# Attention with expert layers on one core: V's high and low parts as one 128-column moving operand, summed by VectorE

## The chip, the cores and the metric

The kernel runs on one core of a Trainium2 chip. The metric is the device time of one execution in microseconds; a comparison takes the median of several runs. A profile is one execution taken by the hardware profiler. Its engines are TensorE (PE, with its weight loads as PEld), VectorE (DVE), ScalarE (ACT), GpSimd (POOL) and SyncE (SP), which here issues the DMAs.

## The reference

Attention over 4 batches of 8 heads, 576 positions and 64 values a head, with a position bias from a small network, and then a two-layer network on the result of all heads side by side (the expert layers).

```python
scores = scale * np.matmul(q, k.transpose(0, 1, 3, 2))
...
scores = scores + bias.transpose(2, 0, 1)[None, :, :, :]
scores = scores - np.max(scores, axis=-1, keepdims=True)
attn = np.exp(scores)
attn = attn / (np.sum(attn, axis=-1, keepdims=True) + 1e-09)
return np.matmul(attn, v).astype(np.float32)
...
h = np.maximum(x @ w_in, 0.0)
return (h * h @ w_out).astype(np.float32)
```

All inputs and the output are float32.

## The kernel before

**Tiling.** Two batches are worked on together (b = 0, 1), so p = 0, 1 is the pair of batches. The query rows of a pair are cut into five blocks c: c = 1 to 4 hold 128 rows of each batch, c = 0, the tail, the last 64 rows of both. A step is one (p, c, h): one head of one block. There are 80 steps, in the order of blocks in ORDER; the first two blocks, (0, 0) and (0, 3), work in float32 (f32c), the other eight in fp16. To keep the accuracy of float32 with fp16 matmuls, each operand is split into a high and a low part, and a product is the sum of three: high times high, high times low, low times high.

**A step of an fp16 block.** qk forms the scores of the head in the PSUM tile sc (L361 for the tail, L367 and L373 otherwise). softmax_a adds the bias and takes the row maximum on VectorE (L388, the score pass), and ScalarE takes the exponential (L394). softmax_b makes the fp16 parts a (high on ScalarE, low on POOL, L420 and L421), 1152 columns a batch: 576 high, 64 low of the last 64 keys and 512 low. A transposing DMA (L423) turns them into at, nine tiles of 128 keys a batch; the fifth holds high and low parts of the last 64 keys together. at and a have two buffers each.

**The product with V** (pv, L442 to L471) comes LAG = 3 steps later. V of a head is v_t, two planes: z = 0 high, z = 1 low, each with five tiles of 128 keys a batch and 64 columns. For each batch half there are 14 matmuls (L458), each with a weight load of its own: tiles 0 to 4 of at times high V and times low V, tiles 5 to 8 times high V. All go to the same 64 columns of the PSUM tile pv, which is one bank (ps_pv has one buffer) and is full after four heads. Then VectorE evacuates it (L470): it multiplies the four heads of each batch half by the reciprocal of the sums and writes x, the 512 columns of all heads. finish_x, at the end of a block, scales x, splits it into fp16 parts xh, and a transposing DMA makes xt.

**The expert layers** of a block are eight units. g1 (L512) is 24 matmuls with 256 columns (128 for the tail) into hp, followed by ScalarE, VectorE and POOL work (L518 to L522); g2 (L535) is 12 matmuls with 512 columns (6 for the tail) into o. They run inside the steps of later blocks, one unit a step, and after the last step for the rest. In the first half, the bias tables are made between them: hg (L282 on VectorE, some on ScalarE), its matmuls bp (L309) and their copies be.

**Order.** Each step calls qk, softmax_a, softmax_b, an expert unit and pv of an earlier head. A scheduler then orders each engine's instructions, and each engine takes its own in that order; the DMAs stand in one queue (SPq).

Of the kernel before, what the change touches and what calls it, by code (L numbers as in the profile page):

```python
# [49 lines left out]
def tile_attention_moe(  # L50
# [11 lines left out]
    nc = tc.nc  # L62
# [366 lines left out]
    def pv(p, c, h):  # L429
        at = st_.pop((p, c, h, "t"))  # L430
        f32 = (p, c) in f32c
        vt = v32[h].rearrange("p (j d) -> p j d", d=D) if f32 else v_t[p, h].rearrange("p z (j d) -> p z j d", d=D)
        if h % 4 == 0:
            pv_t[p, c] = ps_pv.tile([128, 512], F32, tag="pv", name="pv")
        po = pv_t[p, c]
        nb = 2 if c else 1
        for b in range(2):
            if c:
                o = ((h % 4) * 2 + b) * 64
                dst = po[:, o:o + 64]  # L440
            else:
                o = (h % 4) * 64  # L442
                dst = po[64 * b:64 * b + 64, o:o + 64]
            if f32:
# [9 lines left out]

            terms = [(blk, z, blk) for blk in range(5) for z in range(2)] + [(5 + blk, 0, blk) for blk in range(4)]
            for n, (ab, vz, blk) in enumerate(terms):
                lhsT = at[:, 9 * b + ab, :] if c else at[:, ab, 64 * b:64 * b + 64]
                nc.tensor.matmul(out=dst, lhsT=lhsT, rhs=vt[:, vz, 5 * b + blk, :], start=(n == 0), stop=(n == 13),  # L458
                                 tile_position=(0, 0 if c else 64 * b))
        if h % 4 == 3:  # L460
            h0 = h - 3
            if h0 == 0:
                x_t[p, c] = x_p.tile([128, 2, DM], F32, tag="x", name="x")
            x = x_t[p, c]
            su = sums[p, c]
            rd = sm2.tile([128, 4, 2], F32, tag="rd", name="rd")
            nc.scalar.activation(out=rd[:, :, 0:nb], in_=su[:, h0:h0 + 4, 0:nb], func=AF.Identity, bias=eps)
            nc.vector.reciprocal(out=rd[:, :, 0:nb], in_=rd[:, :, 0:nb])
            for b in range(nb):
                nc.vector.tensor_tensor(  # L470
                    out=x[:, b, h0 * 64:h0 * 64 + 256].rearrange("p (h d) -> p h d", d=D),  # L471
                    in0=pv_t[p, c].rearrange("p (h b d) -> p h b d", h=4, d=D)[:, :, b, :] if c
                    else pv_t[p, c][:, 0:256].rearrange("p (h d) -> p h d", d=D),
                    in1=rd[:, :, b:b + 1].to_broadcast([128, 4, D]), op=ALU.mult)
            pv_t.pop((p, c))

# [291 lines left out]
```

## Time and profile before

| what | value |
|---|---|
| runs shown | 692.01, 698.78 and 703.85 us, median 698.78 |
| the profiled execution | 692.05 us, of which span 690.3 |
| mean granted TensorE clock | 0.951 |
| PE busy | 626.1 us, 91% of the span |
| DVE busy | 415.6 us, 60% |
| ACT, POOL busy | 384.9 and 354.0 us, 56% and 51% |
| chain that ended last | PE 69%, DMA 12%, DVE 8%, issue 4% |

A busy share is over the whole span, and stages differ; the windows give it by stretch. A matmul's printed duration reaches to its modelled end and overlaps with the next, so what a run of matmuls costs is read from the starts. The chain of work is followed back from the last instruction, each step to what released it.

### The profile page before, as it was taken

How to read it: one execution, taken by the hardware profiler on the slowest of the kernel's cores; microseconds unless marked ns; L12 is line 12 of the kernel's file. 1: busy time of each engine (PE TensorE's matmuls, PEld its weight loads, DVE VectorE, ACT ScalarE, POOL GpSimd, SP SyncE). 2: the span in 40 equal slices, each digit the busy share in tenths (PEclk: the TensorE clock that was granted, in tenths of full speed). 3: DMA queues.
4: the chain of work that ended last, by engine and by line, in shares of the span. 5: the costliest groups of instructions: out<-in, count | busy, mean ns of one | idle time of the engine just before them, and what ended most of it. 6: DMA issues, size and time to landing. Idle time of an engine off the chain costs nothing.

```text
span 690.3 us, 15578 instructions
## 1 busy us (share of the span) xinstructions
PE 626.1 (91%) x6048; PEld 402.7 (58%) x6048; DVE 415.6 (60%) x830; ACT 384.9 (56%) x854; POOL 354.0 (51%) x369
## 2 busy tenths in 40 slices
PE   4087668899989999999999999999987999999997
PEld 1044335677555555666666676666664766676664
DVE  7458898998966694577657543436448446424120
ACT  6286666778866465765755633445575656431211
POOL 3416544587646445656865644445555664632221
PEclk9586787999999999999999999999998999999999
DMA  8868876576897677899998886459699779451000
GB/s 294 230 190 249 259 230 195 174 210 189 189 203 166 139 171 161 186 197 210 224 183 133 163 168 122 109 104 169 130 207 185 157 144 162 85 120 31 31 1 31
DMA packets 207721, 112.17 MB, mean 162 GB/s; under 512 B 168224, under 2 KB 184608, under 8 KB 207648
## 3 DMA queue, kind: packets, MB, share of 16 engines
q1 hardware_dynamic: 207648, 111.19, 69.9%
q8 instruction: 47, 0.77, 0.5%
q14 instruction: 26, 0.21, 0.1%
HBM read 55.44 MB, written 15.61 MB: 103 GB/s over the span
## 4 chain that ended last, share of the span: by engine, by line
PE 69%; DMA 12%; DVE 8%; issue 4%; ACT 3%; POOL 2%; SPq 0%; DVEq 0%; ACTq 0%; POOLq 0%
PE hp L512 23%; PE o L535 23%; PE pv L458 6%; DMA at<-a 6%; PE sc L373 5%; PE bp L309 3%; PE pv L451 3%; DMA stg<-kd 3%; DVE hg L282 2%; DMA xt<-xh 1%; PE tp L406 1%; PE sc L367 1%; PE sc L361 1%; DMA stg<-w_out 1%; DVE s L388 1%
## 5 line engine op out<-in xcount | busy, mean ns | idle before, releaser
L512 PE MATMUL hp<-xt,winH 128*128 128x256 f16 (+1 forms) x1280 | 195.8, 263 | 1.9 <-DMA xt<-xh 1.9
L535 PE MATMUL o<-woutH,g 128*128 128x512 f16 x576 | 186.2, 382 | 0.6 <-ACT o L542 0.6
L512 PE MATMUL hp<-xt,winL 128*128 128x256 f16 (+1 forms) x640 | 162.0, 262 | 0.0
L512 PEld LDWEIGHTS <-winH 128*128 128x128 f16 x1280 | 116.2, 98 | 36.5 <-issue 17.7
L535 PEld LDWEIGHTS <-g 128*128 128x128 f16 x864 | 83.5, 98 | 92.5 <-issue 8.9
L520 DVE TENSOR_TENSOR r<-hp,r 128x512 f32<-128x512 f32 (+1 forms) x80 | 50.7, 634 | 133.8 <-ACT r L518 133.8
L421 POOL TENSOR_TENSOR a<-s,a 128x1024 f16<-128x1024 f32 (+1 forms) x64 | 130.1, 2032 | 0.0
L522 POOL TENSOR_TENSOR g<-r,g 128x512 f16<-128x512 f32 (+1 forms) x80 | 86.4, 1080 | 80.6 <-DVE g L127 78.4
L388 DVE CUSTOM_DVE_ANT_0 s<-sc,bt 128x576 f32<-128x576 f32 x144 | 103.4, 751 | 38.7 <-PE sc L373 24.9
L394 ACT ACTIVATE s<-s,nm 128x576 f32<-128x576 f32 x144 | 111.4, 774 | 6.9
L535 PE MATMUL o<-woutL,g 128*128 128x512 f16 x288 | 110.0, 382 | 0.0
L392 ACT ACTIVATE nm<-mx,esc 128x1 f32<-128x1 f32 x144 | 41.1, 286 | 120.9 <-DVE mx L388 120.7
L420 POOL TENSOR_TENSOR a<-s,a 128x128 f16<-128x128 f32 (+1 forms) x64 | 28.3, 442 | 141.9 <-ACT a L123 130.6
L123 ACT ACTIVATE a<-s 128x1152 f16<-128x1152 f32 (+1 forms) x64 | 70.5, 1102 | 51.7 <-DMA at<-a 50.4
L518 ACT ACTIVATE r<-hp 128x512 f32<-128x512 f32 (+1 forms) x80 | 43.1, 538 | 60.1 <-PE hp L512 60.0
L458 PEld LDWEIGHTS <-at 128*128 128x128 f16 (+1 forms) x1792 | 60.6, 100 | 23.7 <-issue 8.2
L282 DVE TENSOR_SCALAR hg<-tab_t,nb 128x464 f32<-128x464 f32 (+17 forms) x102 | 62.4, 665 | 9.8 <-PE bp L309 9.6
L458 PE MATMUL pv<-v,at 128*128 128x64 f16 (+1 forms) x1792 | 64.4, 194 | 3.9 <-DMA at<-a 3.9
L512 PEld LDWEIGHTS <-winL 128*128 128x128 f16 x640 | 62.7, 98 | 6.4 <-issue 0.4
L309 PE MATMUL bp<-hg,w2s 128*32 128x288 f32 (+17 forms) x352 | 48.1, 547 | 9.1 <-ACT be L325 5.0
L373 PE MATMUL sc<-k,q 64*128 64x512 f16 x384 | 54.8, 391 | 0.0
L451 PEld LDWEIGHTS pv<-v,at 128*64 128x64 f32 (+3 forms) x320 | 36.1, 181 | 16.8 <-issue 10.7
(71 smaller groups left out, 674.4 us busy)
## 6 DMA issues: line engine op xcount, KB each, us to landing
bt<-biasd SPq DMA_DIRECT2D x64, 288.0 KB, 3.3
stg<-w_in SPq DMA_DIRECT2D x16, 512.0 KB, 4.3
stg<-w_out SPq DMA_DIRECT2D x16, 512.0 KB, 4.5
stg<-kd SPq DMA_DIRECT2D x16, 288.0 KB, 3.9
bt<-biasd SPq DMA_DIRECT2D x32, 144.0 KB, 3.4
qst<-qd SPq DMA_DIRECT2D x32, 128.0 KB, 3.3
out<-o SPq DMA_DIRECT2D x16, 256.0 KB, 2.4
v<-vd SPq DMA_DIRECT2D x8, 320.0 KB, 7.4
```

The source lines that it names most:

```text
L123: nc.scalar.activation(out=out, in_=in_, func=AF.Copy, scale=scale)
L282: nc.vector.tensor_scalar(ht, tab_t[:, 0:dlen(G)], scl[:, n:n + 1], nb1, op0=ALU.mult, op1=ALU.max)
L309: nc.tensor.matmul(out=bp[32 * t:32 * t + 32, 0:d1 - d0], lhsT=w2s, rhs=ts_[t][:, d0:d1], start=True, stop=True, tile_position=(0, 32 * t))
L373: nc.tensor.matmul(out=sc[:, 1024 * b:1024 * b + 512], lhsT=qt[r, qz, qs], rhs=kt[r, z, 64 * b:64 * b + 512], start=(n == 0), stop=(n == 2 ...
L388: nc.vector.tensor_tensor_reduce(s[:, 576 * b:576 * b + 576], sc[:, 960 * b:960 * b + 576], bt, inv, -3.0e38, ALU.add, ALU.max, mx[:, b:b ...
L394: nc.scalar.activation(out=sl, in_=sl, func=AF.Exp, bias=nm[:, b:b + 1], accum_out=su[:, h, b:b + 1])
L421: nc.gpsimd.tensor_tensor(av[:, :, 640:1152], ev[:, :, 0:512], av[:, :, 0:512], op=ALU.subtract)
L451: nc.tensor.matmul(out=dst, lhsT=lhsT, rhs=vt[r, 5 * b + blk, :], start=(blk == 0), stop=(blk == 4), tile_position=(0, 0 if c else 64 * b))
L458: nc.tensor.matmul(out=dst, lhsT=lhsT, rhs=vt[:, vz, 5 * b + blk, :], start=(n == 0), stop=(n == 13), tile_position=(0, 0 if c else 64 * b))
L512: nc.tensor.matmul(out=hp[:, f * T:f * T + T].rearrange("p (b t) -> p b t", b=nb), lhsT=wt[:, k, c0:c0 + 128], rhs=xt[:, 0:nb, z * 4 + k, ...
L522: nc.gpsimd.tensor_tensor(g[:, 1, 0:2 * T], r[:, 0:2 * T], g[:, 0, 0:2 * T], op=ALU.subtract)
L535: nc.tensor.matmul(out=blk["o"][b], lhsT=g[:, z, c0:c0 + 128], rhs=wt[:, 2 * u + f, :], start=(u == 0 and f == 0 and z == 0 and wt is wout ...
```

## The change

In the fp16 blocks, the high and the low part of a tile of V are one moving operand of 128 columns (two pieces of 64). Tiles 0 to 4 of at are each loaded once and multiplied with both; the result is two planes of 64 columns side by side. Tiles 5 to 8 go to the first plane as before. So a batch half has 9 matmuls in place of 14: 5 with 128 columns and 4 with 64. A head takes twice the room in the PSUM tile pv, whose bank is now full after two heads. After each second head, VectorE adds the two planes while it moves them to x (the new tensor_reduce, one for each batch half), and after four heads the multiplication by the reciprocal sums runs on x in place, from SBUF. The tile x is taken at the second head of a block in place of the fourth. The two float32 blocks work as before.

```diff
--- before.py
+++ after.py
@@ -430,17 +430,19 @@
         at = st_.pop((p, c, h, "t"))
         f32 = (p, c) in f32c
         vt = v32[h].rearrange("p (j d) -> p j d", d=D) if f32 else v_t[p, h].rearrange("p z (j d) -> p z j d", d=D)
-        if h % 4 == 0:
+
+        nh, w = (4, D) if f32 else (2, 2 * D)
+        if h % nh == 0:
             pv_t[p, c] = ps_pv.tile([128, 512], F32, tag="pv", name="pv")
         po = pv_t[p, c]
         nb = 2 if c else 1
         for b in range(2):
             if c:
-                o = ((h % 4) * 2 + b) * 64
-                dst = po[:, o:o + 64]
+                o = ((h % nh) * 2 + b) * w
+                dst = po[:, o:o + w]
             else:
-                o = (h % 4) * 64
-                dst = po[64 * b:64 * b + 64, o:o + 64]
+                o = (h % nh) * w
+                dst = po[64 * b:64 * b + 64, o:o + w]
             if f32:
                 for blk in range(5):
                     r = slice(0, 128 if blk < 4 else 64)
@@ -452,27 +454,42 @@
                                      tile_position=(0, 0 if c else 64 * b))
                 continue
 
-            terms = [(blk, z, blk) for blk in range(5) for z in range(2)] + [(5 + blk, 0, blk) for blk in range(4)]
-            for n, (ab, vz, blk) in enumerate(terms):
-                lhsT = at[:, 9 * b + ab, :] if c else at[:, ab, 64 * b:64 * b + 64]
-                nc.tensor.matmul(out=dst, lhsT=lhsT, rhs=vt[:, vz, 5 * b + blk, :], start=(n == 0), stop=(n == 13),
-                                 tile_position=(0, 0 if c else 64 * b))
+            for n in range(9):
+                lhsT = at[:, 9 * b + n, :] if c else at[:, n, 64 * b:64 * b + 64]
+                pos = (0, 0 if c else 64 * b)
+                if n < 5:
+                    nc.tensor.matmul(out=dst.rearrange("p (z d) -> p z d", z=2), lhsT=lhsT, rhs=vt[:, :, 5 * b + n, :],
+                                     start=(n == 0), stop=(n == 8), tile_position=pos)
+                else:
+                    nc.tensor.matmul(out=dst[:, 0:D], lhsT=lhsT, rhs=vt[:, 0, 5 * b + n - 5, :],
+                                     start=False, stop=(n == 8), tile_position=pos)
+        if h == (3 if f32 else 1):
+            x_t[p, c] = x_p.tile([128, 2, DM], F32, tag="x", name="x")
+        x = x_t[p, c] if (p, c) in x_t else None
+        if not f32 and h % 2 == 1:
+
+            for b in range(nb):
+                src = po.rearrange("p (h b z d) -> p h b d z", h=2, b=2, z=2)[:, :, b, :, :] if c else \
+                    po[:, 0:256].rearrange("p (h z d) -> p h d z", h=2, z=2)
+                nc.vector.tensor_reduce(x[:, b, (h - 1) * 64:(h + 1) * 64].rearrange("p (h d) -> p h d", d=D), src,
+                                        axis=AX.X, op=ALU.add)
+            pv_t.pop((p, c))
         if h % 4 == 3:
             h0 = h - 3
-            if h0 == 0:
-                x_t[p, c] = x_p.tile([128, 2, DM], F32, tag="x", name="x")
-            x = x_t[p, c]
             su = sums[p, c]
             rd = sm2.tile([128, 4, 2], F32, tag="rd", name="rd")
             nc.scalar.activation(out=rd[:, :, 0:nb], in_=su[:, h0:h0 + 4, 0:nb], func=AF.Identity, bias=eps)
             nc.vector.reciprocal(out=rd[:, :, 0:nb], in_=rd[:, :, 0:nb])
             for b in range(nb):
-                nc.vector.tensor_tensor(
-                    out=x[:, b, h0 * 64:h0 * 64 + 256].rearrange("p (h d) -> p h d", d=D),
-                    in0=pv_t[p, c].rearrange("p (h b d) -> p h b d", h=4, d=D)[:, :, b, :] if c
-                    else pv_t[p, c][:, 0:256].rearrange("p (h d) -> p h d", d=D),
-                    in1=rd[:, :, b:b + 1].to_broadcast([128, 4, D]), op=ALU.mult)
-            pv_t.pop((p, c))
+                xo = x[:, b, h0 * 64:h0 * 64 + 256].rearrange("p (h d) -> p h d", d=D)
+                if not f32:
+                    xi = xo
+                elif c:
+                    xi = po.rearrange("p (h b d) -> p h b d", h=4, d=D)[:, :, b, :]
+                else:
+                    xi = po[:, 0:256].rearrange("p (h d) -> p h d", d=D)
+                nc.vector.tensor_tensor(out=xo, in0=xi, in1=rd[:, :, b:b + 1].to_broadcast([128, 4, D]), op=ALU.mult)
+            pv_t.pop((p, c), None)
 
     moe = deque()
     blocks = {}
```


On TensorE the matmuls of a head stand as one run before and after, and from the fourth head of the second fp16 block on the runs follow each other almost as before: scores of a head, g1, g2, product with V of an earlier head. Only heads 6 and 7 of a block (in the last block heads 4 and 5) stand with at most scores between them. In the first fp16 block, (0, 2), expert units and bias matmuls are placed otherwise: between its heads 1 and 2 there now stand a score product, six matmuls of g2 and four of bp, where there were a score product, six of g2 and none.

VectorE, first place: around head 3 of the first fp16 block (L388 is the score pass on sc, hg the bias tables, r the first layer's result, x from pv the evacuation). Before:

```order
L282 TENSOR_SCALAR hg<-tab_t,nb_131 128x576 x3
L388 ISA s,mx<-sc,bt 128x576
L388 ISA mx 128x1
L388 ISA s,mx<-sc,bt 128x576
L388 ISA mx 128x1
L470 TENSOR_TENSOR x<-pv,rd 128x256
L520 TENSOR_TENSOR r<-hp,r 128x512
L470 TENSOR_TENSOR x<-pv,rd 128x256
L388 ISA s,mx<-sc,bt 128x576
L388 ISA mx 128x1
```

After, with the lines of the changed kernel (L474 is the new reduce, L491 the multiplication, L537 the former L520):

```order
L388 ISA s,mx<-sc,bt 128x576
L388 ISA mx 128x1
L282 TENSOR_SCALAR hg<-tab_t,nb_131 128x576 x3
L474 TENSOR_REDUCE x<-pv 128x128 x2
L537 TENSOR_TENSOR r<-hp,r 128x512
L491 TENSOR_TENSOR x<-x,rd 128x256 x2
L388 ISA s,mx<-sc,bt 128x576
L388 ISA mx 128x1
L388 ISA s,mx<-sc,bt 128x576
L388 ISA mx 128x1
```

The reduce stands behind the bias tables of 576 columns and ahead of r, and both multiplications stand ahead of the score passes, where they stood on both sides of r.

VectorE, second place: the end of the block (1, 1), while the scores of the tail block are at work (ax, cc and xh belong to finish_x). Before:

```order
L388 ISA s,mx<-sc,bt 128x576
L388 ISA mx 128x1
L470 TENSOR_TENSOR x<-pv,rd 128x256 x2
L487 TENSOR_REDUCE ax<-x 128x2
L489 TENSOR_SCALAR ax<-ax 128x1 x2
L490 RECIPROCAL cc<-ax 128x2
L495 TENSOR_SCALAR xh<-x,cc 128x512
L388 ISA s,mx<-sc,bt 128x576
L388 ISA mx 128x1
L496 SCALAR_TENSOR_TENSOR xh<-x,cc,xh 128x512
```

After:

```order
L388 ISA s,mx<-sc,bt 128x576
L388 ISA mx 128x1
L474 TENSOR_REDUCE x<-pv 128x128 x2
L491 TENSOR_TENSOR x<-x,rd 128x256 x2
L504 TENSOR_REDUCE ax<-x 128x2
L506 TENSOR_SCALAR ax<-ax 128x1 x2
L388 ISA s,mx<-sc,bt 128x576
L388 ISA mx 128x1
L507 RECIPROCAL cc<-ax 128x2
L512 TENSOR_SCALAR xh<-x,cc 128x512
L537 TENSOR_TENSOR r<-hp,r 128x512
```

The reduces were put in ahead of the multiplications, and the score pass that stood after xh now stands ahead of it.

## Rows read from the trace of the kernel before

**Rows 1.** windows by engine, columns named in the first line, 180 to 625 us
```profile
core 0: us, PE busy (x) PEld busy (x) DVE busy (x) ACT busy (x) POOL busy (x), PEclk, DMA share, GB/s
180.00:260.00 80.00, 76.32 (x783) 43.26 (x780) 60.60 (x110) 51.75 (x116) 40.48 (x37) 1.00 0.79 174
345.00:505.00 160.00, 160.00 (x1704) 107.13 (x1703) 79.30 (x171) 82.66 (x179) 84.64 (x87) 1.00 0.75 145
505.00:535.00 30.00, 24.16 (x332) 15.67 (x330) 21.34 (x45) 18.21 (x44) 16.58 (x15) 0.93 1.00 193
535.00:625.00 90.00, 90.00 (x960) 62.52 (x959) 41.44 (x94) 46.73 (x99) 45.70 (x38) 0.98 0.65 128
```

**Rows 2.** TensorE's timeline: start, duration, engine, line, operation; one step of the second half
```profile
491.05 0.98 PE L458 MATMUL pv<-v,at 128*128 128x64 f16 x28
491.86 0.33 PE L367 MATMUL sc<-kz,q 128*128 128x128 f16 x3
492.13 0.82 PE L373 MATMUL sc<-k,q 64*128 64x512 f16 x6
492.88 0.28 PE L512 MATMUL hp<-xt,winH 128*128 128x128 f16 x2
...
494.23 0.38 PE L535 MATMUL o<-woutH,g 128*128 128x512 f16 x1
...
496.82 0.57 PE L458 MATMUL pv<-v,at 128*128 128x64 f16 x14
```

**Rows 3.** the chain of work, piece by piece: start, duration, what; two heads in a row
```profile
607.67 1.63 PE pv L458 x56
```

**Rows 4.** TensorE's groups by form: busy us, mean ns of one, idle before
```profile
L458 PE MATMUL pv<-v,at 128*128 128x64 f16 x1568 | 56.6, 193 | 3.9 <-DMA at<-a 3.9
L458 PE MATMUL pv<-v,at 128*64 128x64 f16 x224 | 7.8, 198 | 0.0
```

**Rows 5.** TensorE's timeline, one head of the tail block
```profile
421.62 0.97 PE L458 MATMUL pv<-v,at 128*64 128x64 f16 x28
422.52 0.91 PE L361 MATMUL sc<-k,q 128*128 128x512 f16 x6
```

**Rows 6.** VectorE's groups by form, the evacuation and the reduces
```profile
L470 DVE TENSOR_TENSOR x<-pv,rd 128x256 f32<-128x256 f32 x36 | 13.8, 416 | 6.8 <-PE pv L458 6.7
L487 DVE TENSOR_REDUCE ax<-x 128x2 f32<-128x1024 f32 x8 | 9.7, 1216 | 0.2
L487 DVE TENSOR_REDUCE ax<-x 128x1 f32<-128x512 f32 x2 | 1.4, 686 | 0.1
```

**Rows 7.** VectorE's timeline at the end of a block
```profile
410.68 0.74 DVE L470 TENSOR_TENSOR x<-pv,rd 128x256 f32<-128x256 f32 x2
411.45 1.22 DVE L487 TENSOR_REDUCE ax<-x 128x2 f32<-128x1024 f32 x1
```

**Rows 8.** waits of the DMA queue: us in total, times, longest
```profile
SPq L423 <- PE pv L458: 68.4, 28, 4.9
```

**Rows 9.** the chain of work at the end of the first fp16 block
```profile
251.29 0.98 DVE xh L496
252.38 3.08 DVE hg L282 x3
255.46 3.13 DMA xt<-xh
...
259.99 3.25 DMA xt<-xh
...
263.29 2.79 PE hp L512 x24
```

**Rows 10.** the chain of work at a later block end
```profile
522.83 3.62 DMA xt<-xh
...
527.87 2.60 DVE xh L496
530.47 0.67 DVE s L388
...
532.36 1.40 PE sc L373 x6
```


## Prediction

> **What bounds the kernel now.** I read the windows first: per stretch of the span, how long each engine was busy. From 345 to 505 us and from 535 to 625 us TensorE is busy 100% of the time at full granted clock or nearly so, and VectorE 50% and 46% [rows 1]. These 250 us hold most of the products with V that the change rewrites. From 180 to 260 us (the first block in fp16, while bias tables are still made) VectorE is at 76% and TensorE leaves 3.7 us of 80 idle; from 505 to 535 us TensorE leaves 5.8 us of 30 idle and VectorE is at 71% [rows 1]. So what counts is TensorE's time per head, and VectorE's only in those two stretches.
>
> Next, TensorE's timeline of one step [rows 2]. The product with V of a head starts at 491.05 us, the scores of a later head at 491.86, 24 matmuls of the first expert layer at 492.88, 12 of the second at 494.23, and the next product with V at 496.82. No idle time stands on any of these rows: the distance from one start to the next is what a group costs, since the durations printed overlap. So a head's 28 matmuls cost 0.81 us. The chain of work shows two heads in a row: 56 matmuls, 1.63 us, 29.1 ns each [rows 3]. The same step prices wider moving operands, each with its own weight load: 24 matmuls with 128 columns take 1.35 us, 56.25 ns each, and 12 with 512 columns 2.59 us, 216 ns each [rows 2]. That is 0.42 to 0.45 ns a column from 64 to 512 columns: the columns are paid for, the number of instructions hardly.
>
> **TensorE's part.** A head of the 56 with 128 query rows per batch (1568 matmuls [rows 4], 28 each) now issues 10 matmuls of 128 columns and 8 of 64. Before: 28 x 29.1 = 815 ns. After: 10 x 56.25 + 8 x 29.1 = 795 ns. That is 20 ns a head, 1.1 us for 56. The 8 heads of the tail block (224 matmuls [rows 4], weights of 64 columns) cost 0.90 us now, 32.1 ns a matmul [rows 5]. With 56.25 ns for the wide ones they would cost 10 x 56.25 + 8 x 32.1 = 819 ns, 81 ns less, 0.6 us for 8. The term is **-1.7 us**, though 640 of 1792 matmuls go.
>
> The doubled matmul itself is not in the trace. If it cost no more than a narrow one, a head would save 10 x 29.1 = 291 ns, 64 heads 18.6 us. The other end is the three 128-column matmuls of the scores, 0.27 us from 491.86 to 492.13, 90 ns each [rows 2]: a head would cost 10 x 90 + 8 x 29.1 = 1133 ns, 318 more, +20.3 us. I take 56.25: the row has the same columns, a weight load per matmul, and 24 in a row, where the group of three ends in a change to weights of half the rows. The point from which the change costs time on TensorE is twice 29.1, 58.2 ns: the estimate lies just below it.
>
> Here a rule speaks against the change. The step shows 56.25 ns for a matmul of 128 columns with its weight load [rows 2]. The Trainium skill, "TensorE: Matmul & The Clock Gate", section "Back-to-back issue gap", gives about 81 ns sustained for 128 columns in a stream of weight loads and matmuls, and about 56 ns only for matmuls in isolation; by it a head would cost 10 x 81 + 233 = 1043 ns, and 64 heads +14.6 us in place of -1.7. The trace agrees with the page's lower figure, in a stream with weight loads.
>
> **VectorE's part.** Added: one reduce per batch half and pair of heads, 7 blocks x 4 pairs x 2 + 4 in the tail block = 60, each 256 values in and 128 out from PSUM. Nothing of this form runs now. Two rows meet: the present evacuation reads 256 values of PSUM in 416 ns; the reduces over 1024 and 512 values, 1216 and 686 ns, give 1.035 ns a value and so 421 ns at 256 [rows 6]. I take 0.42, 0.84 us for a pair. Low end 0.37 (two evacuations back to back, 0.74 us [rows 7]); high end 0.69, if the strided read costs what 512 values do. Sum 25 us (22 to 41). The multiplication by the reciprocal sums stays, 30 of 36 now reading SBUF in place of PSUM; I leave it at 0.42, and if that read were free it would give back at most 30 x 0.42 = 13 us of busy time. VectorE goes from 415.6 us to about 441.
>
> In the two stretches in which TensorE is full this is hidden: VectorE idles there for 80.7 and 48.6 us [rows 1] and gets about 25 x 250 / 445 = 14 us. Two covers must hold. First, the one PSUM bank of the product with V is now full after two heads, so every second head waits for the reduce. By the loop a score product and an expert unit stand between those heads: in [rows 2] 4.96 us from the end of one product to the start of the next, against 0.84. The shortest cover is in the first fp16 block, between heads 1 and 2: scores 1.02 us and six second-layer matmuls 1.3 us, 2.3 us without the bias products. If VectorE came later than that, TensorE would stand. Second, the reduce stands ahead of the next head's score pass on VectorE. That pass waits for the scores anyway, 1.02 us, so 0.84 us fits; at heads 3 and 7 the multiplication (0.74) comes before it too, and the pass is some 0.6 us late. Behind it wait the exponential, the fp16 split and the transposing DMA, whose result is needed three steps later; that DMA stands 68.4 us in all, 28 times, for a product with V to free its buffer [rows 8]. A pass 0.6 us late thus only shortens that wait. Without this cover it would be 16 x 0.6 = 10 us.
>
> **What shows.** At the end of a block the reduces stand in the path from the last product with V to the transposed activations (xt). For most block ends TensorE has older expert work and never idles. On the chain that ended last it shows twice: VectorE's xh, then two transposes to 263.29 us, and again from 522.83 us to the scores at 532.36 [rows 9, 10]. Each gets one pair more: 2 x 0.84 = **+1.7 us** (0 where the DMA is late anyway, up to 3.3 with reduce and multiplication both delayed). In the first fp16 block 8 reduces, 3.4 us, fall on a VectorE at 76% that shares the path with TensorE; I count half, **+1.7 us** (0 to 7.1: all of it, and the 3.7 us that TensorE idles there now once more, since expert units are moved around there).
>
> Sum: -1.7 + 1.7 + 1.7 = +1.7 us. The profiled execution took 692.05 us (span 690.3), so 693.8. The three runs shown are 692.01, 698.78 and 703.85; on their median the sum is 700.5. The profiled execution and one run lie at the low end, so I put the forecast between the two, at **697 us**: no change that can be measured (2%, 13.8 us, is about what a measurement of this kernel can tell).
>
> **The rivals.**
> - *The wide matmul costs 81 ns or more in this place* (slower). Mechanism: weights and a split moving operand (two pieces of 64) don't overlap as in the 24 matmuls of rows 2. Price +14.6 us at 81 and +20.3 at 90, so 707 to 712 against 692.05. It decides from 80 ns (13.8 us / 640 + 58.2). For it: the group of three at 90 ns. Against: the 24 also read a moving operand of their own and hold 56.25. Chance 0.05.
> - *The bank becomes the wait.* VectorE reaches the reduce late, TensorE stands at the 32 pair starts. In the first fp16 block alone, 4 starts of 1 to 2 us give 4 to 8 us, 696 to 700; chance 0.15. At 0.43 us on every start it passes 13.8 us, 706 and more; chance 0.03, since covers are near 5 us.
> - *All of VectorE's work is hidden*: -1.7 us, 690.3. For it: only two block ends lie on the chain. Chance 0.19.
> - *The moved expert units fill the stall at 505 to 535 us*: up to -5.8 us, 686. Chance 0.06.
> - *Wide matmuls are as cheap as narrow ones*: -18.6 us, 673. Against it: cost per column is constant in rows 2. Chance 0.03.
> The forecast as summed, -1 to +5 us about it, has the rest, 0.49.
>
> **How the numbers follow.** Faster by over 2%: the last rival and a little of the one before it, 0.04. Slower by over 2%: 0.05 + 0.03 and a little for delays that add up, 0.09. Within 2%: 0.87. The range, 689 to 706 us, goes from the hidden case on the lowest run to the bank case on the median; it leaves out the two ends of the wide matmul's price and half of what the runs scatter.
>
> **What would show it.** In the profile after: 18 matmuls of a head in 0.79 us (right) or over 1 us (first rival); reduces of 0.4 us, 60 of them, and VectorE near 441 us; TensorE still at 100% in the steps of the second half, with no wait for VectorE ahead of an even head; the chain's block ends about 0.8 us longer. A wait of TensorE for the reduce, in total over 5 us, would make the second rival right. The forecast is wrong if the wide matmul leaves 50 to 65 ns, or if the first fp16 block, 177 to about 250 us now, changes its length by more than 7 us.

## The result and the profile after

The changed kernel takes 700.51 us (median of 20 runs, 695.33 to 708.88) against 695.79 us (20 runs, 689.94 to 703.85) of the kernel before beside it: a ratio of 1.0068, 95% interval 1.0043 to 1.0094. It is slower by about 4.7 us. The forecast was no change that can be measured; the sum behind it, 1.7 us more than before, is 3.0 us too low.

The windows of the profile after, in the columns of [rows 1]; the execution's span is 699.0 us (690.3 before):

```profile
180.00:260.00 80.00, 76.48 (x648) 39.97 (x646) 59.20 (x113) 48.79 (x110) 41.13 (x38) 0.96 0.77 165
345.00:505.00 160.00, 158.16 (x1426) 105.39 (x1425) 89.39 (x193) 81.79 (x178) 85.89 (x89) 1.00 0.69 144
505.00:535.00 30.00, 28.18 (x334) 18.48 (x332) 20.47 (x50) 20.66 (x49) 16.87 (x17) 1.00 0.90 191
535.00:625.00 90.00, 86.62 (x807) 58.90 (x806) 51.98 (x113) 50.43 (x108) 50.38 (x43) 0.98 0.74 144
```

From 345 to 505 us TensorE is still nearly full, and VectorE has 10 us more to do than in [rows 1]. From 535 to 625 TensorE now has 3.4 us of idle time where it had none. Most of it is not new: one score product waits 3.30 us for the score pass, and before it waited 3.91 us, but earlier, inside the window from 505 to 535. After, and before:

```profile
541.88 0.45 PE L367 MATMUL sc<-kz,q 128*128 128x128 f16 x3 [3.30 <-DVE mx L388]
```

```profile
531.88 0.48 PE L367 MATMUL sc<-kz,q 128*128 128x128 f16 x3 [3.91 <-DVE mx L388]
```

TensorE's timeline: a head with 128 query rows per batch (314.06 to 314.85), and a head of the tail block (433.01 to 433.84):

```profile
314.06 0.44 PE L461 MATMUL pv<-v,at 128*128 128x128 f16 x5
314.34 0.28 PE L464 MATMUL pv<-v,at 128*128 128x64 f16 x4
314.45 0.44 PE L461 MATMUL pv<-v,at 128*128 128x128 f16 x5
314.73 0.28 PE L464 MATMUL pv<-v,at 128*128 128x64 f16 x4
314.85 0.33 PE L367 MATMUL sc<-kz,q 128*128 128x128 f16 x3
...
433.01 0.47 PE L461 MATMUL pv<-v,at 128*64 128x128 f16 x5
...
433.84 0.88 PE L361 MATMUL sc<-k,q 128*128 128x512 f16 x5
```

The 18 matmuls of a head take 0.79 us (0.815 before), those of a tail head 0.83 us (0.90 in [rows 5]). Five wide ones take 0.28 us from start to start, 56 ns each.

VectorE's groups after (busy us, mean ns of one | idle before), the page's line of busy times, and three waits after (us in total, times, longest):

```profile
L474 DVE TENSOR_REDUCE x<-pv 128x128 f32<-128x256 f32 x60 | 22.7, 416 | 17.8 <-PE pv L464 17.7
L491 DVE TENSOR_TENSOR x<-x,rd 128x256 f32<-128x256 f32 x30 | 22.6, 786 | 0.1
L491 DVE TENSOR_TENSOR x<-pv,rd 128x256 f32<-128x256 f32 x6 | 2.3, 412 | 0.0
```

```profile
PE 629.1 (90%) x5408; PEld 399.5 (57%) x5408; DVE 441.1 (63%) x890; ACT 384.3 (55%) x854; POOL 355.9 (51%) x369
```

```profile
PE sc L367 <- DVE mx L388: 16.2, 7, 4.8
...
PEld bp L309 <- DVE x L474: 0.2, 1, 0.2
...
SPq L423 <- PE pv L464: 64.5, 27, 4.7
```

The first of these waits in the kernel before:

```profile
PE sc L367 <- DVE mx L388: 10.9, 3, 4.5
```

The reduces are as priced, 0.416 us from PSUM. The 30 multiplications that now read the sum from SBUF are not: 786 ns in the mean, against 412 ns for the six (of the f32 blocks) that still read PSUM, and 416 ns in [rows 6]. VectorE's 441.1 us are the forecast figure only by chance: 22.7 us of reduces and some 11 us by which the multiplications are stretched are more than the 25.5 us by which it rose from 415.6, so other work fell by about 8 us. TensorE hardly ever waits for the reduce (0.2 us). It waits more for the score pass (mx), 16.2 us at 7 places in place of 10.9 us at 3: a score product can't start until the pass of an earlier head has read its banks. Two of these places in either profile, 5.6 and 7.0 us, lie in the first 177 us, where the kernels do the same; behind them it is 10.7 us at 5 places in place of 3.9 us at one.

Where the time goes is read from the start of each head's product with V, as its lateness against the profile before. The first 177 us, which the change does not touch, differ from execution to execution (the profiled executions of e6, e7 and e10 below are slow ones, and there they are 10 to 12 us longer), so I count from the first fp16 product (177.7 us before). The profile before is of an execution 3.7 us below the median of its runs, so lateness against it is larger than the loss in the medians. At that first product the changed kernel is 1.1 us late, at head (0,1,1) 5.6, at (0,1,2) 10.2, at (0,1,6) 10.7, at the last head 8.8. Through the full stretch from (1,1,2) to (1,4,5) it gains 0.85 us, 0.02 to 0.03 us a head and 0.07 in the tail block: the wide matmuls' gain, as forecast. The loss lies ahead of it, in the first two fp16 blocks and their ends. Larger steps, of 5 and 10 us at heads (0,2,2) and (0,4,0), are mostly taken back by the heads next to them; the sharpest that stays is 4.65 us, at (0,1,2). VectorE's timeline there, ahead of the score pass, and TensorE's:

```profile
317.65 0.63 DVE L537 TENSOR_TENSOR r<-hp,r 128x512 f32<-128x512 f32 x1
318.20 1.68 DVE L512 TENSOR_SCALAR xh<-x,cc 128x512 f16<-128x512 f32 x1
319.80 0.50 DVE L127 TENSOR_SCALAR g<-r 128x512 f16<-128x512 f32 x1
320.23 0.73 DVE L513 SCALAR_TENSOR_TENSOR xh<-x,cc,xh 128x512 f16<-128x512 f32 x1
322.70 1.27 DVE L139 SCALAR_TENSOR_TENSOR v<-stg,v 128x640 f16<-128x640 f32 x1 [1.74 <-POOL v L125]
323.90 0.74 DVE L388 CUSTOM_DVE_ANT_0 s<-sc,bt 128x576 f32<-128x576 f32 x1
```

```profile
321.76 0.28 PE L464 MATMUL pv<-v,at 128*128 128x64 f16 x4
325.38 0.33 PE L367 MATMUL sc<-kz,q 128*128 128x128 f16 x3 [3.34 <-DVE mx L388]
```

And the same place before, on VectorE:

```profile
312.15 1.95 DVE L127 TENSOR_SCALAR g<-r 128x512 f16<-128x512 f32 x1
314.02 0.74 DVE L388 CUSTOM_DVE_ANT_0 s<-sc,bt 128x576 f32<-128x576 f32 x1
...
316.31 1.27 DVE L139 SCALAR_TENSOR_TENSOR v<-stg,v 128x640 f16<-128x640 f32 x1 [0.85 <-POOL v L125]
```

Before, the score pass (L388) stands ahead of the cast of V (L139) that waits for GpSimd, and the second half of x's scaling is done by 311.5 us. After, this half (L512, L513) and the cast, with a wait of 1.74 us, stand directly ahead of the pass: the end of block (0,4) runs later, and the scheduler has put its pieces into VectorE's fixed order at another place. TensorE stands 3.34 us.

Then its clock falls. From 326.9 to 330.3 us the granted clock is 0.50, the level of 1.2 GHz; before, it is 1.00 (2.4 GHz) all through this place. The window of that stretch, TensorE's timeline after from g1 to the product with V, and the one before from the scores to g2:

```profile
326.90:330.30 3.40, 3.40 (x18) 2.42 (x17) 2.81 (x8) 3.31 (x8) 2.22 (x3) 0.50 1.45 300
```

```profile
326.39 0.39 PE L529 MATMUL hp<-xt,winH 128*128 128x256 f16 x2
...
330.69 0.38 PE L552 MATMUL o<-woutH,g 128*128 128x512 f16 x1
...
333.28 0.44 PE L461 MATMUL pv<-v,at 128*128 128x128 f16 x5
```

```profile
316.33 0.33 PE L367 MATMUL sc<-kz,q 128*128 128x128 f16 x3
...
317.84 0.39 PE L512 MATMUL hp<-xt,winH 128*128 128x256 f16 x2 [0.42 <-DMA xt<-xh]
...
320.47 0.38 PE L535 MATMUL o<-woutH,g 128*128 128x512 f16 x1
```

The 24 matmuls of g1 take 4.30 us (326.39 to 330.69) in place of 2.63 (317.84 to 320.47), 1.67 us more. From 325.38 us to the product with V at 333.28 us TensorE has no idle time, so that product does not wait for its transposing DMA. The step is 3.34 us of standing and 1.67 us of slower clock, less the 0.42 us for which TensorE waited before, ahead of g1: 4.6 of the 4.65 us. In e1, e3, e4, e7, e9 and e11 below, TensorE stands 2.5 to 3.5 us for the pass at this place too, and each time the granted clock is 0.50 for 3.4 us from about then on.

### The profile page after: what moved, and what is told of

Its sections match the earlier page's. It is cut to its first block, busy times and chain, and to the rows that moved or that the text cites. A ratio compares the mean times of both kernels' runs of the same rounds, so it can differ in the third digit from the quotient of the medians.

```text
span 699.0 us, 14369 instructions
## 1 busy us (share of the span) xinstructions
PE 629.1 (90%) x5408; PEld 399.5 (57%) x5408; DVE 441.1 (63%) x890; ACT 384.3 (55%) x854; POOL 355.9 (51%) x369
## 4 chain that ended last, share of the span: by engine, by line
PE 40%; DVE 5%; DMA 5%; issue 2%; ACT 2%; POOL 2%; POOLq 0%; DVEq 0%; ACTq 0%
PE o L552 16%; PE hp L529 16%; DMA at<-a 3%; PE pv L461 3%; PE sc L373 3%; DMA xt<-xh 2%; DVE s L388 1%; PE pv L464 1%; ACT a L123 1%; PE sc L361 1%; DVE x L491 1%; POOL a L421 1%; PE sc L367 1%; DVE g L127 0%; DVE xh L512 0%
## 5 line engine op out<-in xcount | busy, mean ns | idle before, releaser
L537 DVE TENSOR_TENSOR r<-hp,r 128x512 f32<-128x512 f32 (+1 forms) x80 | 50.8, 635 | 124.1 <-ACT r L535 123.6
L388 DVE CUSTOM_DVE_ANT_0 s<-sc,bt 128x576 f32<-128x576 f32 x144 | 103.5, 751 | 18.6 <-PE sc L373 12.4
L309 PE MATMUL bp<-hg,w2s 128*32 128x288 f32 (+17 forms) x352 | 51.8, 557 | 7.6 <-ACT be L325 3.2
L461 PE MATMUL pv<-v,at 128*128 128x128 f16 (+1 forms) x640 | 54.3, 220 | 2.0 <-DMA at<-a 2.0
L461 PEld LDWEIGHTS <-at 128*128 128x128 f16 (+1 forms) x640 | 41.2, 99 | 21.8 <-issue 7.8
L453 PEld LDWEIGHTS pv<-v,at 128*64 128x64 f32 (+3 forms) x320 | 34.7, 176 | 16.8 <-issue 10.7
```

The source lines that it names most:

```text
L309: nc.tensor.matmul(out=bp[32 * t:32 * t + 32, 0:d1 - d0], lhsT=w2s, rhs=ts_[t][:, d0:d1], start=True, stop=True, tile_position=(0, 32 * t))
L388: nc.vector.tensor_tensor_reduce(s[:, 576 * b:576 * b + 576], sc[:, 960 * b:960 * b + 576], bt, inv, -3.0e38, ALU.add, ALU.max, mx[:, b:b ...
L461: nc.tensor.matmul(out=dst.rearrange("p (z d) -> p z d", z=2), lhsT=lhsT, rhs=vt[:, :, 5 * b + n, :], start=(n == 0), stop=(n == 8), tile_ ...
L537: nc.vector.tensor_tensor(rr, hp[:, 0:2 * T], rr, op=ALU.mult)
```

## The experiments

Each ratio is to the kernel before on the same chip. "Early" is the lateness gained from the first fp16 product to that of head (0,1,6), "late" from there to the last head, both in us and read from one profiled execution. The changed kernel has +9.6 early and -1.9 late in one execution, +6.3 and -1.6 in another (e1): a difference of 3 us between single executions means little.

| run | ratio (95%) | VectorE busy us | early | late |
|---|---|---|---|---|
| e1 changed kernel again | 1.0064 (1.0032 to 1.0096) | 441.9 | +6.3 | -1.6 |
| e2 no sum | 0.9979 (0.9934 to 1.0023) | 418.5 | +2.6 | -4.0 |
| e3 narrow matmuls | 1.0144 (1.0101 to 1.0187) | 446.0 | +6.0 | +4.2 |
| e4 first block old | 1.0085 (1.0055 to 1.0114) | 447.8 | +4.5 | +0.7 |
| e5 no multiplication | 0.9941 (0.9904 to 0.9979) | 427.7 | +1.9 | -4.4 |
| e6 copies for reduces | 1.0106 (1.0061 to 1.0152) | 437.5 | +8.4 | -1.0 |
| e7 multiplied from PSUM | 1.0052 (1.0012 to 1.0091) | 448.0 | +6.4 | -2.2 |
| e8 two blocks old | 1.0039 (1.0004 to 1.0074) | 438.6 | +1.2 | +6.3 |
| e9 45 reduces more | 1.0176 (1.0132 to 1.0220) | 457.6 | +9.4 | +0.9 |
| e10 GpSimd multiplies | 1.0178 (1.0148 to 1.0207) | 425.4 | +8.1 | +5.3 |
| e11 before, 56 reduces more | 1.0030 (1.0000 to 1.0060) | 437.2 | +4.5 | -0.2 |
| e12 cast behind | 1.0136 (1.0091 to 1.0180) | 439.7 | +8.9 | -1.2 |
| e13 before, cast ahead | 1.0053 (1.0024 to 1.0082) | 418.5 | +3.1 | +0.1 |
| e14 two ends | 1.0163 (1.0119 to 1.0208) | 444.6 | +9.1 | +1.4 |
| e15 two ends, early | 1.0135 (1.0094 to 1.0176) | 437.9 | +7.6 | -0.2 |

TensorE's clock is part of these numbers. From the first fp16 product to the last head the granted clock is 0.50 for 6.8 us in the profile before (530.9 to 537.7 us) and for 13.6 us in the one after. e2 and e5, the only two runs that are not slower, have no such stretch there; the others have 3.4 to 13.6 us. At the 1.67 us that 3.4 us cost above, the 6.8 us of the profile before are worth 3.3 us (an estimate); with the wide matmuls' 0.85 us this is about the late gain of e2 and e5. How much of each run's loss is waiting and how much is the slower clock was not parted.

**The two halves of the change.** Theory A: VectorE's added work is not hidden, and the wide matmuls cost nothing. Theory B: the loss is the changed order of work in the first fp16 block. e1 is the changed kernel once more. e2 keeps the wide matmuls and the bank of two heads and takes VectorE's added work away; e3 does the opposite; e4 leaves the first fp16 block as it was.

> The changed kernel once more, beside the kernel before on the same chip: every theory expects a ratio of about 1.007 (measured 1.0068). Its profile is a second look at where the time is lost. Theory A (VectorE: 25 us of reduces, and the multiplication, which now reads two SBUF operands and took up to 2.35 us in place of 0.42 while POOL worked) expects the multiplications to be stretched again, some 1 to 2 us each in about half of the pairs. Theory B (the order of the first fp16 block, in which expert units and bias matmuls were moved) expects the heads (0,4,0) to (0,4,3) some 3 to 6 us later than before again, and nothing lost after them.

> The wide matmuls and the bank of two heads stay, but no planes are added: the multiplication takes the first plane straight from PSUM after each second head, so the part of low V is left out of the result. VectorE has 60 multiplications of 128 values from PSUM in place of 60 reduces and 30 multiplications from SBUF. The order on TensorE stays close to that of the changed kernel, the first fp16 block too. Theory A expects the whole loss gone: ratio to before 0.997 to 1.000. Theory B expects the loss to stay: 1.004 to 1.007.

```diff
-                nc.vector.tensor_reduce(x[:, b, (h - 1) * 64:(h + 1) * 64]..., src, axis=AX.X, op=ALU.add)
+                nc.vector.tensor_tensor(out=x[:, b, (h - 1) * 64:(h + 1) * 64]..., in0=hi,
+                    in1=rd_t[p, c][:, i4:i4 + 2, b:b + 1].to_broadcast([128, 2, D]), op=ALU.mult)
```

> The 28 narrow matmuls of before, but into two planes, with the reduces, the bank of two heads and the multiplication from SBUF of the changed kernel. The order on TensorE is close to that of before, the first fp16 block too. Theory A expects a loss as large as that of the change and TensorE's gain of 1.7 us missing: ratio 1.007 to 1.010. Theory B expects 1.000 to 1.003.

```diff
-            for n in range(9):
+            for n, (ab, vz, blk) in enumerate(terms):   # 14 narrow matmuls, into two planes
```

> The change in all fp16 blocks but the first, (0,2), which works as before; the order on TensorE is almost that of before. Theory A expects 7 of 8 parts of VectorE's work and most of the loss: 1.003 to 1.006. Theory B expects no loss and TensorE's gain: 0.997 to 1.000.

```diff
-        nh, w = (4, D) if f32 else (2, 2 * D)
+        old = (p, c) == (0, 2)
+        nh, w = (4, D) if f32 or old else (2, 2 * D)
```

With the wide matmuls and without the sum (e2) nothing is lost; with the sum and without the wide matmuls (e3) more is lost than in the whole change. So the loss is VectorE's side, and e2 and e1 differ by 0.85%, 5.9 us. Theory A's price was too low, though: e3 and e4 lose more than it expected (1.007 to 1.010 and 1.003 to 1.006). The order of the first fp16 block is not it: e4 has almost that block's order of before and is no faster than e1. The step at head (0,1,2) is in e1, e3 and e4 (+3.7 to +4.7 us) and not in e2 (-0.5).

**Which part of VectorE's work.** The multiplication from SBUF is stretched. VectorE's timeline at a block end, and GpSimd's at the same time:

```profile
526.70 0.76 DVE L474 TENSOR_REDUCE x<-pv 128x128 f32<-128x256 f32 x2
527.37 2.69 DVE L491 TENSOR_TENSOR x<-x,rd 128x256 f32<-128x256 f32 x2
```

```profile
527.41 2.36 POOL L421 TENSOR_TENSOR a<-s,a 128x1024 f16<-128x1024 f32 x1
```

Two multiplications take 2.69 us in place of 0.84 while GpSimd's subtraction runs beside them. Over all 30, one takes (duration ns, min/median/max):

```profile
L491 DVE TENSOR_TENSOR x<-x,rd x30: 408/422/2353, 209.9 to 631.1; 128x256 f32<-128x256 f32 x30
```
 The Trainium skill, "SBUF — State Buffer", section "Who interferes with whom", says that a VectorE instruction with two SBUF inputs contends with a GpSimd instruction that reads SBUF, and that tensor_reduce never does on this chip. The trace agrees on both: the same multiplication takes 412 ns from PSUM; the reduces stay at 416 ns from PSUM and, in e7, at 422 ns from SBUF. Theory P makes this wait the cause, theory R the reduces. e5 leaves the multiplication out, e6 puts a copy of half the size in place of the reduce, e7 multiplies first, from PSUM, and reduces from SBUF, and e8 leaves blocks (0,2) and (0,4) as they were.

> The changed kernel without the multiplication by the reciprocal sums in the fp16 blocks (that part of the computation is left out: x stays unnormalised); the 60 reduces stay. It parts the two pieces of VectorE's added time. Theory P (the multiplication is the culprit: from SBUF it has two SBUF inputs and waits while GpSimd runs an operation that reads SBUF, up to 2.35 us instead of 0.42): no jump of +4 us between heads (0,1,1) and (0,1,2), and a ratio of 0.996 to 1.001 to the kernel before (692 to 696 us), since TensorE's 1.7 us are left as a gain. Theory R (the reduces' 22.7 us are the culprit, by their mere amount): the jump stays at about +4 us and the ratio lies at 1.004 to 1.007.

```diff
                 if not f32:
-                    xi = xo
+                    continue
```

> The changed kernel with each reduce replaced by a copy of the high part's product alone (the low part of V is left out of the sum); the multiplication from SBUF stays. The copies handle half the values: about 60 x 0.25 to 0.29 us = 15 to 17 us instead of 22.7. Theory P (multiplication waiting for GpSimd): the multiplications still average 0.7 to 0.9 us with single ones above 2 us, the jump of +4 us stays, ratio 1.004 to 1.007 (697 to 700 us). Theory R (reduces): about a third of the reduces' time goes, ratio 1.000 to 1.004, jump at most +2.5 us.

```diff
-                nc.vector.tensor_reduce(x[:, b, (h - 1) * 64:(h + 1) * 64]..., src, axis=AX.X, op=ALU.add)
+                nc.vector.tensor_copy(x[:, b, (h - 1) * 64:(h + 1) * 64]..., src)   # src: the high plane
```

> The whole computation, in another order: after each second head one multiplication takes all 256 values of a batch (high and low products of two heads) from PSUM into a scratch tile in SBUF, and a reduce from SBUF sums the two parts into x. No VectorE operation of the product with V then has two SBUF inputs, but VectorE does more: 60 x (0.42 + 0.42) = 50 us instead of the 22.7 + 24.7 measured in the changed kernel. Theory P (the waits for GpSimd): multiplications at 0.42 us throughout, no jump of +4 us, ratio 0.998 to 1.002 (693 to 697 us), so at or below the kernel before. Theory R (the amount of VectorE's work): ratio 1.006 to 1.010, as slow as the changed kernel or slower.

```diff
+                nc.vector.tensor_tensor(out=xm, in0=po.rearrange("p (h b y) -> p h b y", h=2, b=2)[:, :, b, :] if c
+                    else po[:, 0:256].rearrange("p (h y) -> p h y", h=2),
+                    in1=rd_t[p, c][:, i4:i4 + 2, b:b + 1].to_broadcast([128, 2, 2 * D]), op=ALU.mult)
-                nc.vector.tensor_reduce(x[...], src, axis=AX.X, op=ALU.add)
+                nc.vector.tensor_reduce(x[...], xm.rearrange("p h (z d) -> p h d z", z=2), axis=AX.X, op=ALU.add)
```

> The change everywhere but in blocks (0,2) and (0,4), the first two in fp16. It tests the place. If the loss arises at the end of block (0,4), where the second part of the low products and a cast that waits for GpSimd come to stand ahead of a score pass: no jump between heads (0,1,1) and (0,1,2), ratio 0.998 to 1.003 (TensorE's gain of 24 narrow-query heads x 0.02 + 8 tail heads x 0.08 us = 1.1 us, against up to +1.6 us at head (1,1,2)). If every block end pays alike, two of eight ends are free: ratio 1.004 to 1.006.

```diff
+        old = (p, c) in ((0, 2), (0, 4))
```

e5 fits theory P: no step, and faster than before, more than expected even. e7 speaks against it. VectorE's groups in e7:

```profile
L484 DVE TENSOR_REDUCE x<-xm 128x128 f32<-128x256 f32 x60 | 25.3, 422 | 1.2
L480 DVE TENSOR_TENSOR xm<-pv,rd 128x256 f32<-128x256 f32 x60 | 25.3, 422 | 15.0 <-PE pv L466 14.0
```

No multiplication is stretched (422 ns), VectorE is as busy as in any kernel so far (448.0 us), and the loss is that of the changed kernel, step of +4.3 us included. So the wait for GpSimd is not needed for the loss; that it costs as time on VectorE, as any other time would, is argued and not shown apart. Theory R falls too: e6 spares 8 us on the sums (60 copies take 14.6 us) and is slower still; its multiplications are stretched further, 28.4 us in all in its one profile. Its ratio lies above both expectations, and its step (theory P: +4 us, theory R: at most +2.5) fits neither: at (0,1,2) it has +0.4, and +4.5 two and three heads later. e8 lies between its two expectations: it loses little early (+1.2) and has no step, as it should if the place is the first two fp16 blocks, but loses later in its one profile (+6.3), and its runs are 0.39% slower.

**The amount.** What remains of these is theory A: it is the amount of VectorE's work in the stretches where its queue is full. e9 adds reduces to the changed kernel, e11 to the kernel before, and e10 takes the multiplication to GpSimd.

> The changed kernel with every reduce of the head pairs 0-1, 2-3 and 4-5 issued a second time into a scratch tile (its result is not used): 45 more reduces of 0.42 us from PSUM, 19 us more on VectorE, none at a block's end and none that has two SBUF inputs. Theory A (what counts is the amount of VectorE's work, since its queue is in order and casts, score passes and evacuations share it): so far 25 us between the run without the multiplication and the changed kernel cost 7 us, 0.28 us for each, so 19 us more give +5 us, a ratio of 1.011 to 1.018. Theory P (only the multiplications' waits for GpSimd) and theory E (only the longer chain at a block's end) both say as the changed kernel, 1.005 to 1.008.

```diff
+                if h < 7:
+                    xe = xe_p.tile([128, 128], F32, tag="xe", name="xe")
+                    nc.vector.tensor_reduce(xe..., src, axis=AX.X, op=ALU.add)
```

> The whole computation; the 30 multiplications of the fp16 blocks are done by GpSimd instead of VectorE, the reduces stay. VectorE's work falls by 24.7 us to about that of the run without the multiplication; GpSimd gets 30 x 1.0 to 1.2 us = 30 to 36 us, and a block's end waits for two of them, 2.1 us instead of 0.84. Theory A: ratio 0.992 to 0.998, below the kernel before. Rival: GpSimd, for which VectorE's casts of k and v already wait at block ends, becomes the wait: ratio 1.001 to 1.008, with more idle time ahead of the casts on VectorE.

```diff
-                nc.vector.tensor_tensor(out=xo, in0=xi, in1=rd[...]..., op=ALU.mult)
+                eng = nc.vector if f32 else nc.gpsimd
+                eng.tensor_tensor(out=xo, in0=xi, in1=rd[...]..., op=ALU.mult)
```

> The kernel before, with its narrow matmuls, its bank of four heads and its multiplication from PSUM, and 56 reduces of 256 values from PSUM into a scratch tile besides, one per batch after each second head (all fp16 blocks but the tail block; their result is not used): 23.5 us more on VectorE at the places where the changed kernel sums, and nothing else. Theory A: 23.5 us lie between the runs with +10 and +22 us of VectorE work and above, so +3.5 to +5.5 us, a ratio of 1.004 to 1.008. Theory P (only the multiplications' waits for GpSimd cost): 0.998 to 1.002.

```diff
+        if c and not f32 and h % 2 == 1:
+            for b in range(nb):
+                nc.vector.tensor_reduce(xe..., po[:, o:o + 256]..., axis=AX.X, op=ALU.add)
```

```profile
L475 DVE TENSOR_REDUCE x<-pv 128x128 f32<-128x256 f32 x60 | 24.4, 416 | 16.6 <-PE pv L465 16.6
L495 DVE TENSOR_TENSOR x<-x,rd 128x256 f32<-128x256 f32 x30 | 22.9, 783 | 0.0
L479 DVE TENSOR_REDUCE xe<-pv 128x128 f32<-128x256 f32 x45 | 18.6, 414 | 0.0
```

Those are e9's groups: 18.6 us more of plain reduces, none at a block's end, none that waits for GpSimd, cost 1.1% more than e1, inside theory A's range, and against P and against a theory that counts block ends alone. e11 is weaker: 23.6 us of reduces in the kernel before cost 0.30% (0 to 0.60), less than the 0.4 to 0.8% expected and about half of the change's loss; the interval leaves room for either. Its profile has the step at (0,1,2) too, +3.9 us, without any multiplication from SBUF. e10 was a miss: VectorE falls to 425.4 us, and the kernel is as slow as e9. GpSimd's group, and two of VectorE's waits:

```profile
L492 POOL TENSOR_TENSOR x<-x,rd 128x256 f32<-128x256 f32 x30 | 20.7, 708 | 5.6 <-DVE x L474 5.4
```

```profile
DVE v L139 <- POOL v L125: 20.7, 8, 6.6
...
DVE ax L505 <- POOL x L492: 8.7, 8, 2.8
```

GpSimd does a multiplication in 0.71 us, in place of the 1.0 to 1.2 expected, but now VectorE waits 8.7 us for it at the block ends (ax). The 20.7 us for GpSimd's part of V prove little: they are 18.5 us in the kernel before and 15.7 in the changed one. The expectation's rival fits, at more than twice its price; that GpSimd is what costs here was not tested further.

**The order.** Theory O makes the order of VectorE's queue the cause. In every kernel from e1 to e11 with a step at head (0,1,2), the waiting cast of V stands ahead of the score pass on VectorE; in every one without, behind it. e12 is meant to move only that in the changed kernel, e13 does the reverse in the kernel before, e14 and e15 treat the next block end too.

> The changed kernel, the whole computation, with one thing moved: the scores of head (0,1,4) get an earlier place, so that on VectorE the score pass and a cast of K stand ahead of the second cast of V that waits for GpSimd after block (0,4). The reduces, the multiplications and their number stay. Theory O (what costs is that the score pass stands in VectorE's queue behind a cast that waits): the jump of +4 to +4.7 us between heads (0,1,1) and (0,1,2) falls below +1.5 us and the ratio to 0.999 to 1.003. Theory A (the amount of VectorE's work alone): the jump and the ratio stay, 1.005 to 1.008.

```diff
-            qk(p, c, h)
-            softmax_a(p, c, h)
+            with later(-40 if t == 36 else 0):
+                qk(p, c, h)
+                softmax_a(p, c, h)
```

> The kernel before with none of the change: only the scores of head (0,1,4) get a later place, so that the cast of V that waits for GpSimd stands ahead of the score pass on VectorE, as in the changed kernel. Theory O: a jump of +2 to +4.5 us between heads (0,1,1) and (0,1,2) and a ratio of 1.003 to 1.006 without any added work. Theory A: no jump above 0.5 us, ratio 0.999 to 1.001.

 (`later(20 if t == 36 else 0)`, in the kernel before)

> As the run with the cast behind, and besides, after the next block, (0,1), the score pass of head (1,1,4) stands ahead of the second block-end scaling xh that waits for a transposing DMA. Theory O: the step of +0.9 to +1.15 us between heads (1,1,1) and (1,1,2) goes too, ratio 0.997 to 1.002, 0.5 to 1.2 us below the run with the cast behind. Theory A: 1.005 to 1.008.

 (`later(-40 if t in (36, 44) else 0)`)

> As the run with two ends, but both score passes stand as early as they can, ahead of the whole second scaling of x as well. The expert units that wait for that scaling come later by its 1.2 us; backlog of eight units should cover it. Theory O: no jump above 0.5 us at either place, ratio 0.996 to 1.001. If instead the scaling's lateness is what the end then waits for: 1.002 to 1.006.

 (`later(-2000 if t in (36, 44) else 0)`)

e12's step at (0,1,2) is gone (-0.5 us), and yet the kernel is no faster than e1, rather slower. Its timelines, VectorE's and then TensorE's, show where the time went:

```profile
338.54 1.27 DVE L139 SCALAR_TENSOR_TENSOR v<-stg,v 128x640 f16<-128x640 f32 x1 [3.17 <-POOL v L125]
...
341.46 0.75 DVE L474 TENSOR_REDUCE x<-pv 128x128 f32<-128x256 f32 x2
342.12 2.68 DVE L491 TENSOR_TENSOR x<-x,rd 128x256 f32<-128x256 f32 x2
344.72 0.74 DVE L388 CUSTOM_DVE_ANT_0 s<-sc,bt 128x576 f32<-128x576 f32 x1
```

```profile
342.35 0.44 PE L461 MATMUL pv<-v,at 128*128 128x128 f16 x5 [0.53 <-DVE x L474]
...
346.21 0.44 PE L367 MATMUL sc<-kz,q 128*128 128x128 f16 x3 [2.91 <-DVE mx L388]
```

The next cast of V waits longer (3.17 us), and reduce, stretched multiplication and score pass queue up behind it; TensorE waits 0.53 us for the bank and 2.91 us for the pass, three heads later than it stood in the changed kernel. The whole step from (0,1,4) to (0,1,5) is +3.8 us. So in e12 the order decides where the loss shows, not whether there is one. e13 shows that the order alone can also cost: the kernel before, with not one instruction more, loses 0.53%. Its price lies in the range expected, its place does not: the steps are +1.7 us at (0,1,1) and +1.0 at (0,1,3), none at (0,1,2), where the cast does stand ahead of the pass. e14 and e15 are both misses for theory O; no version tried beats the kernel before with the whole computation done.

## Why the prediction was right or wrong

- **The wide matmul, 56.25 ns, and a head at 795 ns: right.** 0.79 us, and 0.83 us in the tail block. In the full stretch the changed kernel gains as forecast, e3 with its narrow matmuls gains nothing there. The rivals at 81 to 90 ns and at the price of a narrow one are refuted.
- **The reduces, 60 x 0.42 us: right** (22.7 us in all). **The bank of two heads becomes the wait: refuted**; TensorE waits 0.2 us for the reduce, and e2 has that bank and loses nothing.
- **The multiplication left at 0.42 us, with bounds only downward: wrong.** It takes 786 (after) and 858 ns (e1) in the mean, some 11 to 13 us more in all, since from SBUF it has two SBUF inputs and waits while GpSimd reads. By e7, which loses about as much without it, this is not the only way to the loss.
- **"The pass is some 0.6 us late", and the late pass "only shortens" the wait of the transposing DMA: this is the step that failed.** The DMA's slack is there; its wait for the product with V is 64.5 us, against 68.4 in [rows 8]. But the DMA is not the only one that waits for the pass. The next score product does too, for the banks that the pass frees, and behind the first fp16 product that wait rose from 3.9 to 10.7 us. The pass is late by as much as stands ahead of it in VectorE's fixed order, which at block ends and at every fourth head is a reduce, a pair of multiplications of up to 2.7 us and casts that wait for GpSimd, not 0.6 us. At the sharpest place TensorE stood 3.34 us, and the clock that fell behind it cost 1.67 us more; the sum has a term for neither. The prediction priced this cover, if lost, at 10 us for 16 such places; measured over the whole kernel, VectorE's added work costs 4.7 + 1.7 = 6.4 us by the medians, with the forecast gain on TensorE, where the sum had 3.4.
- **The place: half right.** Half of the 3.4 us was put on the first fp16 block, which with the next one and its end does carry the loss (+6.3 to +9.6 us ahead of head (0,1,6)); the end of block (0,4), the sharpest step, was not named. The later block end shows +1.1 us at head (1,2,2), near the 0.84 of the sum; it is taken back two heads on, where the granted clock is 0.50 for 3.4 us (541.9 to 545.4) in place of 6.8.
- **The stall at 505 to 535 us filled by moved expert units: hardly.** TensorE's idle time there fell from 5.8 to 1.8 us, but the wait of 3.91 us came again later, as 3.30 us at 541.88; over both windows idle time fell from 5.8 to 5.2 us.
- **The anchor.** 697.0 lay between a low execution and a high median of three; on the median of the 20 runs beside the change the sum gives 697.5, and the time is 700.5.

What stays open: the loss does not follow the amount of VectorE's work in strict proportion. e6 has less of it than e1 and loses more, e11's 23.6 us cost half of what the change costs, and e13 loses without any. Each edit makes the scheduler order all queues anew, and by e13 a new order alone can cost 3.7 us. Amount, order and the clock that falls behind a wait were not parted further; shown is that it is VectorE's part of the change that costs.

## What to carry to other kernels

Work that is added to an engine with 40% idle time is not hidden by that share: ask at each place what stands behind it in that engine's fixed order, list everyone who waits for that (the next product that needs the bank, not only the next step of the data), and price the worst place, not the mean. Read the granted clock behind each long wait: matmuls that run slower after a wait are part of its price. When an operand moves from PSUM to SBUF, look up what else uses SBUF at that time, and bound its price upward too. To split a change in two, run each half alone first: here one pair of runs (e2 and e3) told which engine it was.

## What the runs showed of the hardware

- VectorE's multiplication of 256 values: 412 to 422 ns in the mean from PSUM (singly 406 to 426), and up to 2.35 us from SBUF while GpSimd's subtraction of 1024 values runs (2.1 to 2.7 us). The reduce of 256 values stays at 416 to 422 ns in the mean, from PSUM and from SBUF (e7; at most 430).
- GpSimd multiplies 128 x 256 values in 0.71 us in the mean (e10), 1.7 times VectorE's undisturbed time.
- Matmuls with 128 moving columns in two pieces of 64, each with a weight load of its own, hold 56 ns in a row, as those with one piece do in [rows 2].
- Behind a wait of 3.34 us TensorE's granted clock was 0.50 from 326.9 to 330.3 us, and 24 matmuls with 256 columns took 4.30 us in place of 2.63.
